# Two attention decodes on one core: last scores of a chunk ahead of the value matmuls, and a loop head of the tensor engine without its pin

## The chip, the cores and the metric

The kernel runs on one core of a Trainium2 chip. The metric is the device time of one execution in microseconds (us); I give medians of several executions. Profile times are counted from the start of the span, which is some 1.8 us shorter than the device time of the same execution.

## The reference, cut to what matters

Two single-token attention decodes with batch 4 and head size 128, their outputs side by side:

```python
def _A_ref(x, k_cache, v_cache, wq, wo):        # 32 query heads, 8 key heads, last W = 2048 of 8192 rows
    q = (x @ wq) ...
    scores = einsum("bhqd,bhkd->bhqk", q, k) * Dh ** -0.5
    o = einsum("bhqk,bhkd->bhqd", softmax(scores), v)
    return o.reshape(B, Sq, Hq * Dh) @ wo
def _B_ref(...):                                # the same, 32 key heads, all 8192 rows
    ...
return concatenate([_A_ref(...), _B_ref(...)], axis=-1)
```

"A" is the sliding-window part, "B" the block-cached one. Together they read 587 MB from memory, nearly all of it keys and values of B.

## The kernel before

The work is cut into 72 chunks: 8 of A, then 64 of B. A chunk of B is two heads of one batch row: 128 key tiles and 128 value tiles of 128x128, 4 MB each. For each chunk the tensor engine transposes the key tiles in groups of eight, another engine copies (evacuates) each group from `tr`, a PSUM tile of this kernel, to `kt` (one copy takes 691 ns on the vector engine and 1023 ns on the scalar engine, by the page of before), and the tensor engine multiplies the group with the query (scores). The values of the chunk before are multiplied in the second half of a chunk. Every engine's list of operations is written out by one Python program; repeating stretches, two chunks long, are then turned into loops of the engine's program. So the tensor engine has two loops, one in A (3 turns) and one in B (32 turns).

```python
def keys_part(c):
    if c % 2 == 0: sch.mark()                  # a loop turn begins here
    for g in range(ch["NG"]):                  # 16 groups in B
        emit_T(ch["s"] + g)                    # 8 transposes, then the evacuation on DVE or ACT
        if g >= SLAG: emit_S(ch["s"] + g - SLAG)   # scores, two groups behind (SLAG = 2)
        ...

def values_part(c, nxt):                       # values of chunk c, and the last two score groups of nxt
    late = list(range(ch["s_last"] + 1 - SLAG, ch["s_last"] + 1))
    todo = {2: lambda: emit_S(late[0]), 5: lambda: scores_last(nxt)} if ch["ab"] == 1 else {...}
    if ch["ab"] == 1:
        todo[10] = lambda: stats_gmax(nxt)                      # maximum over all partitions
        todo[14] = lambda: (stats_bc(nxt), exp_B(nxt))          # broadcast it, exponentials on ACT
    ...
    for g in range(16):
        emit_pv(c, g)                          # 8 value matmuls
        if g in todo: todo[g]()

for c in range(NC):
    if c == NCA: finish_A()                    # between the two loops
    keys_part(c)
    values_part(None if c == 0 else NONE if c == NCA else c - 1, c)
norm_sum(NC - 1); emit_wol()                   # after the loops: sums, output weights,
for g in ...: emit_pv(NC - 1, g)               # values of the last chunk, output
...
sch.emit_looped("pe", e, sems, loop_on(mybir.EngineType.PE, (0, 0)))   # head slots of the two loops
```

In the profile's lines `tr` are the transposes, `sc` the scores, `po` the value matmuls, `ms` small matmuls for maxima, broadcasts and sums, `pbb` the exponentials of B and `fin` the output product; DVE and ACT are the vector and the scalar engine, PEld the tensor engine's weight loads, and SP issues the loads.

A head slot of 0 pins the loop's first instruction to the start of a 256-instruction block of the engine's program; the padding ahead of it is jumped over. The traces show: an instruction packet is 16 KB (17 of them are 0.28 MB on the page of before); stalls by issue in the first passes fall 256 instructions apart. Loads are all issued by one queue, two buffers each for the keys and the values of B: a key load waits for the transposes of two chunks earlier, a value load for the value matmuls of two chunks earlier.

## Time and profile before

| | before |
|---|---|
| median of the first three runs | 1381.0 us (1378.02 to 1381.39) |
| span of the profiled run | 1378.8 us |
| tensor engine busy (PE, matmuls) | 1179.7 us, 86% |
| data queue, share of the 16 DMA engines | 99.4% |
| mean rate | 426 GB/s |

Read it with the DMA first. A load queue that is busy 99.4% of the span leaves only those places where it is not full, and the ends, where no load hides what is done. A tensor engine busy at 86% looks like a near second, but its idle time in the middle is waiting for keys (153.3 us in 58 waits in all). The prediction shows the lines for it.

### The profile page before, as it was taken

Reading aid. Unit: us, or ns where it says so; the run is one execution under the profiler, and the core shown is the slowest. Engines: PE = TensorE matmul, PEld = TensorE weight load, DVE = VectorE, ACT = ScalarE, POOL = GpSimd, SP = SyncE. Lnnn points to the kernel's source line nnn. Section 1 sums busy time; section 2 is a strip of 40 time slices with the busy share of each in tenths; the row PEclk is TensorE's granted clock in tenths of the full one; section 3 lists DMA queues with packets and bytes.
Section 4 is the critical chain, followed back from the end, with each engine's and each line's share of the span. In section 5 each row is a group of like instructions: output and inputs, shape, how many; then the busy total and the mean of one; then the engine's idle time right before and its main releaser. Section 6 shows DMA issues by size and latency. Waiting matters only on the chain.

```text
span 1378.8 us, 59836 instructions
## 1 busy us (share of the span) xinstructions
PE 1179.7 (86%) x27000; PEld 1137.7 (83%) x27001; DVE 656.7 (48%) x1434; ACT 434.8 (32%) x650; POOL 7.3 (1%) x28
## 2 busy tenths in 40 slices
PE   4896898888889888988889888988898889888988
PEld 4885898888888888888888888888887879787987
DVE  1674464444445444444445444444454445444543
ACT  1552333233223322332233233323232323232332
POOL 2000000000000000000000000000000000000000
PEclk9897999999999999999999999999999999999998
DMA  9999999999999999999999999999999999999997
GB/s 400 424 424 432 384 430 436 426 438 429 431 433 427 433 431 435 429 432 433 428 433 434 427 437 429 433 429 432 435 429 435 427 433 432 430 434 430 434 424 318
DMA packets 25254, 587.55 MB, mean 426 GB/s; under 512 B 2816, under 2 KB 2832, under 8 KB 6288
## 3 DMA queue, kind: packets, MB, share of 16 engines
q1 hardware_dynamic: 25208, 587.22, 99.4%
q8 instruction: 17, 0.28, 0.1%
q14 instruction: 5, 0.04, 0.0%
q10 hardware_dynamic: 24, 0.01, 0.0%
HBM read 587.21 MB, written 0.01 MB: 426 GB/s over the span
## 4 chain that ended last, share of the span: by engine, by line
DMA 61%; PE 36%; DVE 1%; issue 1%; ACT 0%; SPq 0%; DVEq 0%; ACTq 0%
DMA kv<-in_B_k_cache_dram 56%; PE tr L406 22%; PE sc L408 9%; PE po L408 2%; DMA kv<-in_B_v_cache_dram 2%; DMA kv<-in_B_wq_dram 2%; PE fin L408 2%; DMA kv<-in_A_k_cache_dram 1%; PE ms L408 1%; DVE sA L525 1%; ACT pba L595 0%; DVE rm L534 0%; DVE sA L523 0%; PE ms L406 0%; DVE zA L681 0%
## 5 line engine op out<-in xcount | busy, mean ns | idle before, releaser
L406 PE MATMUL tr<-identb,kv 128*128 128x128 bf16 x8704 | 701.5, 231 | 163.4 <-DMA kv<-in_B_k_cache_dram 153.3
L476 DVE COPY kt<-tr 128x1024 bf16<-128x1024 bf16 x736 | 502.7, 691 | 454.7 <-PE tr L406 450.2
L406 PEld LDWEIGHTS tr<-identb,kv 128*128 128x128 bf16 x8704 | 555.2, 104 | 186.2 <-DMA kv<-in_B_k_cache_dram 96.0
L474 ACT ACTIVATE kt<-tr 128x1024 bf16<-128x1024 bf16 x352 | 359.3, 1023 | 629.3 <-PE tr L406 629.1
L408 PE MATMUL sc<-qb,kt 128*128 128x64 bf16 x8704 | 449.5, 197 | 0.6 <-DVE gx L555 0.6
L408 PEld LDWEIGHTS sc<-qb,kt 128*128 128x128 bf16 x8704 | 371.8, 101 | 3.4 <-DVE gx L555 1.1
L408 PE MATMUL po<-pbb,kv 128*128 128x64 bf16 x8320 | 296.5, 192 | 6.6 <-issue 3.6
L408 PEld LDWEIGHTS po<-pbb,kv 128*128 128x128 bf16 x8320 | 269.5, 97 | 9.0 <-issue 3.7
L575 ACT ACTIVATE pbb<-sc,negb 64x128 bf16<-64x128 f32 x128 | 51.0, 399 | 298.3 <-DVE negb L562 297.5
L539 DVE TENSOR_REDUCE rm<-sc 64x1 f32<-64x128 f32 x128 | 36.9, 288 | 97.3 <-PE sc L408 96.4
L551 DVE TENSOR_REDUCE gm<-ms 1x2 f32<-1x128 f32 (+1 forms) x72 | 20.1, 279 | 48.5 <-PE ms L406 48.5
L562 DVE COPY negb<-ms 128x1 f32<-128x1 f32 (+1 forms) x72 | 11.4, 158 | 50.2 <-PE ms L408 50.2
L408 PE MATMUL ms<-identf,gx 1*128 1x1 f32 (+1 forms) x144 | 27.5, 258 | 0.8 <-DVE zA L681 0.8
L408 PEld LDWEIGHTS ms<-identf,gx 1*128 1x128 f32 (+1 forms) x144 | 21.4, 185 | 4.7 <-DVE zA L681 0.9
L575 ACT ACTIVATION_READ_ACCUMULATOR pbb<-sc,negb 64x1 f32 x128 | 23.7, 185 | 0.0
L406 PE MATMUL ms<-identf,rm 128*1 128x128 f32 (+1 forms) x72 | 19.7, 274 | 3.4 <-DVE rm L534 3.3
L408 PE MATMUL po<-pba,kv 128*128 128x64 bf16 x512 | 20.3, 199 | 1.6 <-ACT pba L595 1.0
L408 PEld LDWEIGHTS po<-pba,kv 128*128 128x128 bf16 x512 | 17.9, 102 | 4.5 <-ACT pba L595 3.8
L408 PE MATMUL fin<-wos,zB 128*4 128x512 bf16 x64 | 19.0, 378 | 0.0
L555 DVE TENSOR_SCALAR gx<-gm 1x128 f32<-1x128 f32 (+1 forms) x72 | 15.9, 221 | 2.5
L681 DVE CAST zB<-ms 64x8 bf16<-64x8 f32 x64 | 10.5, 163 | 8.9 <-PE ms L408 8.5
L408 PE MATMUL ms<-xT,kv 128*128 128x4 bf16 x256 | 7.1, 166 | 8.2 <-DMA kv<-in_A_wq_dram 4.5
(61 smaller groups left out, 168.1 us busy)
## 6 DMA issues: line engine op xcount, KB each, us to landing
kv<-in_B_k_cache_dram SPq DMA_DIRECT2D x63, 4096.0 KB, 27.2
kv<-in_B_v_cache_dram SPq DMA_DIRECT2D x63, 4096.0 KB, 31.9
kv<-in_A_k_cache_dram SPq DMA_DIRECT2D x8, 2048.0 KB, 13.0
kv<-in_A_v_cache_dram SPq DMA_DIRECT2D x8, 2048.0 KB, 14.8
kv<-in_A_wq_dram SPq DMA_DIRECT2D x1, 4096.0 KB, 12.4
kv<-in_B_wq_dram SPq DMA_DIRECT2D x1, 4096.0 KB, 27.3
wor<-in_A_wo_dram SPq DMA_DIRECT2D x8, 512.0 KB, 9.5
wos<-in_B_wo_dram SPq DMA_DIRECT2D x16, 256.0 KB, 20.4
```

What stands on the lines that cost most here:

```text
L406: sch.add("pe", lambda e: e.transpose(o, l, r), waits, key)
L408: sch.add("pe", lambda e: e.matmul(o, l, r, start=start, stop=stop), waits, key)
L474: sch.add("act", lambda e: e.activation(dst, src, ACTF.Copy), waits=waits, key=("ev", s))
L476: sch.add("dve", lambda e: e.tensor_copy(dst, src), waits=waits, key=("ev", s))
L525: emit = lambda e, src=src, b=b: e.scalar_tensor_tensor(out=t, in0=src, scalar=mk[:, b:b + 1], in1=t, op0=ALU.mult, op1=ALU.add)
L539: sch.add("dve", lambda e, src=src, pp=pp: e.tensor_reduce(out=rm[pp, m, 0:1], in_=src, axis=AX.X, op=ALU.max), waits=[("S", ch["s_last"]) ...
L551: sch.add("dve", lambda e: e.tensor_reduce(out=gm[0:C, m, 0:U], in_=src, axis=AX.X, op=ALU.max), waits=[("trm", c)], key=("gmax", c))
L555: sch.add("dve", lambda e: e.tensor_scalar(out=dst, in0=gv, scalar1=-scale, scalar2=None, op0=ALU.mult), waits=[("gmax", c)], key=("gx", c))
L562: sch.add("dve", lambda e: e.tensor_copy(negb[:, m, 0:C], ms[:, col:col + C]), waits=[("bc", c)], key=("negb", c))
L575: sch.add("act", lambda e, src=src, pp=pp, n=n, u=u: e.activation(probs_of(c)[pp, :, u], src, ACTF.Exp, bias=negb[pp, m, 0:1], scale=scale ...
L681: sch.add("dve", lambda e, src=src, pp=pp: e.tensor_copy(z[pp, :].rearrange("p (r b) -> p r b", r=k), src), waits=[("sm", c)] + free if h ...
```

## The change

The intent is twofold. First, in B, the last two score groups go ahead of most of the value matmuls, and with them the maximum and the exponentials, so that they are ready sooner. Second, the head of the tensor engine's A loop is no longer pinned, and lies wherever the instructions ahead of it end.

```diff
             late = list(range(ch["s_last"] + 1 - SLAG, ch["s_last"] + 1))
-            todo = {2: lambda: emit_S(late[0]), 5: lambda: scores_last(nxt)} if ch["ab"] == 1 else {0: lambda: emit_S(late[0]), 1: lambda: scores_last(nxt)}
             if ch["ab"] == 1:
-                todo[10] = lambda: stats_gmax(nxt)
-                todo[14] = lambda: (stats_bc(nxt), exp_B(nxt))
+                emit_S(late[0])
+                todo = {1: lambda: scores_last(nxt), 6: lambda: stats_gmax(nxt), 10: lambda: (stats_bc(nxt), exp_B(nxt))}
+            else:
+                todo = {0: lambda: emit_S(late[0]), 1: lambda: scores_last(nxt)}
...
-            sch.emit_looped("pe", e, sems, loop_on(mybir.EngineType.PE, (0, 0)))
+            sch.emit_looped("pe", e, sems, loop_on(mybir.EngineType.PE, (None, 0)))
```

## The prediction

Its sum: 1381.0 us, less 1.3 for the order, less 2.5 for the loop head (0.65 x 3.9), is 1377.2. What stands in it of fetching comes from counting in the trace of before: after five stalls the next fetch began 3.6 to 4.5 us later; the "3.6 to 5 us" and the range of slots from 100 to 240 are my estimates from that.

> **What bounds the kernel now.** I read the page first, its slices and its chain, then the stretches of time, then the waits of the tensor engine and the end of the chain in order of time.
>
> ```profile
> PEclk9897999999999999999999999999999999999998
> DMA  9999999999999999999999999999999999999997
> GB/s 400 424 424 432 384 430 436 426 438 429 431 433 427 433 431 435 429 432 433 428 433 434 427 437 429 433 429 432 435 429 435 427 433 432 430 434 430 434 424 318
> ...
> q1 hardware_dynamic: 25208, 587.22, 99.4%
> ```
>
> The data queue is busy 99.4% of the span and moves 424 to 438 GB/s in nearly every slice. 587.2 MB at the 431 GB/s of the long middle is 1362 us of the 1378.8 us span. So only three places are left for a gain: the start (slice 0), slice 4 with 384 GB/s, and the end (slice 39, 318 GB/s). The stretches, as a table, put numbers on the last two:
>
> ```profile
> 137.00:171.00 34.00, 29.85 (x709) 28.84 (x705) 16.29 (x35) 10.38 (x17) 0.00 (x0) 0.95 0.94 382
> 171.00:231.00 60.00, 59.60 (x1493) 58.00 (x1490) 34.37 (x73) 22.16 (x31) 0.00 (x0) 1.00 1.00 431
> 231.00:1330.00 1099.00, 948.00 (x21847) 921.97 (x21847) 517.21 (x1093) 337.35 (x504) 0.00 (x0) 0.93 1.00 431
> ```
>
> The columns are the stretch, its length, busy time of PE, PEld, DVE, ACT and POOL, the granted clock, the DMA share and GB/s. From 231 to 1330 us the tensor engine is busy 948 of 1099 us and idles 151 us; the DMA never idles (share 1.00). The chain agrees: 55.7% of the span is waiting for key loads of B. From 137 to 171 us the DMA delivers 382 instead of 431 GB/s: 34 x (431-382)/431 = 3.9 us of transfer lost. That is the passage from the sliding-window chunks (A) to the block-cached ones (B). The end, in the chain:
>
> ```profile
> 1330.26 31.64 DMA kv<-in_B_v_cache_dram
> ...
> 1363.40 0.43 PE sc L408 x8
> ...
> 1365.11 0.43 PE sc L408 x8
> ...
> 1368.88 0.32 PE ms L408 x2
> ...
> 1369.89 0.46 ACT pbb L575 x2
> ...
> 1371.66 3.76 PE po L408 x128
> ```
>
> Columns: start, duration, what. The values of the last but one chunk land at 1361.9 us. Then the tensor engine does 128 value matmuls of that chunk, the last two score groups (8 matmuls, 0.43 us each), waits for the exponentials, and does the last 128 value matmuls. This end runs on the tensor engine, not on the DMA.
>
> [...] the instruction queue (17 packets, 0.28 MB on the page) makes no block transfer from 72 to 123.5 us, then one at 126.1 us, while the tensor engine stands still from 123.53 to 128.96 us. [...] the trace shows clock 0.50 from 1361.1 to 1367.9 us.
>
> **Part one: order of scores and values.** For every B chunk the second to last score group moves from after three value groups to before the first, the last from after group 5 to after group 1, the global maximum from 10 to 6, and the broadcast with the exponentials from 14 to 10. No instruction is added or removed. The distances between dependent steps stay nearly the same (last scores to maximum: 5 groups either way; maximum to broadcast: 4). The first moved group needs an evacuation which ends about 1.0 us after its transposes; at the old place it had long been done, at the new one it may cost some 0.1 us per chunk. In the middle this goes into the 151 us of idle time, some 2.6 us for each of 57 chunks (1099 us at 19.4 us a chunk). Key buffers are freed by transposes, which do not move; value buffers by the last value matmul, before which as much work stands as ever. So loads are issued at the same times and **the middle gains 0**.
>
> At the end it gains: the first score group (0.43 us) is done while the engine waits for the values (it idles 1358.9 to 1361.9), and the exponentials get five value groups, 40 matmuls, behind which to hide instead of one. They take from the end of the broadcast at 1369.2 to 1370.36, some 1.2 to 1.5 us with the broadcast's copy; 40 matmuls take 40 x 31 ns = 1.25 us at full clock and 2.1 us at half. The wait of 0.98 us (value matmuls done about 1369.41, next matmul 1370.39) shrinks to 0 to 0.3. Sum 0.43 + 0.85 = **1.3 us**. The last values have landed by 1370.3, so the shortened end runs into no new wait.
>
> **Part two: the loop head.** The pin to slot 0 of a fetch block is taken off the A loop; the B loop keeps it. What does this do? A fetch starts about 3.6 to 5 us after the block before it is entered (five stalls that end with a fetch show 3.6 to 4.5 us until the next fetch begins). Counting rows of the tensor engine: the A loop has 859 instructions, what follows it up to the branch to the B loop 175. With the A head at slot 0 the branch sits at 859 + 175 = 1034 = 4 x 256 + 10: the last block is entered only 10 instructions before the jump, so the block of the B head is asked for just as it is needed. Hence the stall:
>
> ```profile
> PE tr L406 <- issue: 6.0, 2, 5.4
> ```
>
> That is, in the waits of the stretch from 100 to 175 us: 6.0 us over 2 times, 5.4 us the longest. This one stall delays the first transposes of B, the key load they release is issued at 141.12 us, and the DMA runs dry: the one hole of 3.9 us above. The first B keys had landed at 123.3 us, so without the stall the engine could start at once.
>
> If the A head starts elsewhere, at slot s, the branch sits at s + 1034, and the block is entered s + 10 instructions before it. For s between roughly 100 and 240 that is 2 us of sequencer time or much more, and the fetch is hidden wholly or mostly. The 5.4 us go, the first loads of B are issued about 4.5 us earlier, and **the hole closes: 3.9 us**, all of it on the path, as the DMA is what limits the rest. Where s is I can only estimate from the times of the early fetches: the block before the A head was entered some 230 to 255 instructions ahead of it. If s is so near to the end of the block that head and boundary coincide, nothing changes. I give 0.65 to the hole closing: 0.65 x 3.9 = **2.5 us** expected.
>
> **Rivals.**
> First, the loads stay as they are, the unpinned head falls on the old place or only the stall's place moves, and just the end gains: 1381.0 - 1.3 = 1379.7 us. For it: my count of s comes close to the boundary. Against it: the pin would then have been without effect.
> Second, the moved scores wait for the evacuation, the tensor engine becomes the bound and loads go out later: at 0.1 us for 64 chunks, 6 us slower if all were exposed. Against it: 2.6 us idle per chunk, and loads that take 27 to 32 us from issue to landing, two to three deep.
> Third, a tensor engine kept busier and earlier scores help the middle: PE busy 86% could tempt one to expect several per cent. Against it: DMA share 1.00 at 431 GB/s over 1099 us.
> Fourth, the clock: at the end the half clock lasted 6.8 us. [...] if the end is at half clock for 3.4 us, it is about 1.5 us shorter, in either kernel. This goes into the range.
>
> **Range and chances.** 1381.0 - 1.3 - 2.5 = 1377.2; I say 1377.0 us. With the hole closed 1375.8, without 1379.7; the three runs of before spread over 3.4 us (1378.02 to 1381.39), so 1373.0 to 1381.0 should hold it 8 times in 10. Two per cent are 27.6 us, seven times all that I found to win: faster 0.01, within 0.98, slower 0.01.
>
> **What would show it.** Part two right: between 120 and 135 us no 5 us stall by issue before the first B transposes, and 137 to 171 us at about 430 GB/s. Wrong: the stall stands, or another of its size shows up in the A chunks. Part one right: one score group before the wait for the last-but-one values, and under 0.3 us between the last value matmul of that chunk and the sums. The middle should show the same 431 GB/s and the same 19.4 us per chunk. The prediction fails if the key loads are issued later in the middle and the DMA share drops below 1.00, or if the middle moves at another GB/s than before.

## The result, and the profile after

The changed kernel takes 1375.43 us (median of 6 runs, 1374.3 to 1375.56); before, over six runs, 1379.64 us. The ratio is 0.9968, 95% interval 0.9955 to 0.9981. (Ratios here are the mean time of one kernel's runs over that of the other's of the same rounds, so not quite the ratio of the medians.) By this ratio it is 4.4 us less, clear of noise, within 2%. The profiled span fell by 5.1 us, from 1378.8 to 1373.7 us.

The page of the changed kernel, rate in the 40 slices and the queue of instruction blocks:

```profile
GB/s 401 423 424 433 426 434 426 437 429 433 429 433 429 432 429 434 428 434 428 434 428 434 429 435 431 431 431 431 431 431 432 430 432 430 432 430 432 430 427 338
...
q8 instruction: 16, 0.26, 0.1%
```

Slice 4 now moves 426 GB/s in place of 384. One block of instructions fewer is fetched, 16 in place of 17. The stretches of the changed kernel, same columns as in the prediction:

```profile
137.00:171.00 34.00, 27.64 (x604) 26.48 (x601) 13.86 (x31) 8.98 (x15) 0.00 (x0) 0.90 1.00 427
171.00:231.00 60.00, 58.84 (x1460) 56.64 (x1457) 33.54 (x74) 22.05 (x34) 0.00 (x0) 1.00 1.00 432
231.00:1325.00 1094.00, 950.31 (x21733) 917.51 (x21734) 515.66 (x1087) 336.45 (x500) 0.00 (x0) 0.93 1.00 431
```

The hole from 137 to 171 us is gone, and the middle moves the same 431 GB/s. What became of the stall ahead of the first B transposes is seen in the order of time (start, duration, the instructions, and in brackets the idle time before them and what ended it), first the kernel before, then the changed one:

```profile
128.97 0.50 PE L406 MATMUL tr<-identb,kv 128*128 128x128 bf16 x3 [5.43 <-issue]
```
```profile
123.41 0.79 PE L406 MATMUL tr<-identb,kv 128*128 128x128 bf16 x11 [0.72 <-DVE outsb L716]
```

The first B transposes start 5.6 us earlier, as soon as their keys have landed. The key load that they release is issued at 134.07 us in place of 141.12 us. From there the lead can be followed by the start of the first transposes of each chunk: chunk 16 starts at 271.32 us in place of 274.31 (3.0 us earlier), chunk 44 at 820.08 in place of 822.97, chunk 70 at 1329.32 in place of 1332.10 (2.8 us). So the middle neither adds to it nor takes much of it.

The remaining 2.3 us of the span come after the values of the last but one chunk have landed. The end of the chain of the changed kernel (start, duration, what):

```profile
1359.14 0.65 PE po L408 x16
1359.79 0.43 PE sc L408 x8
...
1363.78 0.31 PE ms L408 x2
1364.09 1.27 PE po L408 x40
1365.36 0.31 PE ms L408 x2
...
1366.56 3.76 PE po L408 x128
```

One score group stands among the value matmuls in place of two, and forty value matmuls follow the broadcast in place of eight; the sums (`ms`, 1365.36) follow them directly, where there had been 0.98 us of waiting for the exponentials. But 0.43 + 0.98 is 1.4 us, not 2.3. The experiments show where the rest comes from.

One new wait came with the order. In the waits of the changed kernel (total, times, longest):

```profile
PE sc L408 <- ACT kt L474: 12.8, 63, 0.2
```

The moved score group waits 0.2 us for its evacuation in nearly every chunk. The middle does not show it: there the engine waits for keys anyway (133.2 us in 57 waits in all).

### The profile page after: what moved, and what is told of

Read it like the earlier page. It is cut to its first block, busy times and chain, and to the rows that moved or that the text cites. A ratio compares the mean times of both kernels' runs of the same rounds, so it can differ in the third digit from the quotient of the medians.

```text
span 1373.7 us, 59835 instructions
## 1 busy us (share of the span) xinstructions
PE 1184.8 (86%) x27000; PEld 1134.7 (83%) x27001; DVE 656.5 (48%) x1434; ACT 434.8 (32%) x650; POOL 7.3 (1%) x28
## 4 chain that ended last, share of the span: by engine, by line
DMA 59%; PE 37%; DVE 2%; issue 1%; ACT 1%; SPq 0%; DVEq 0%
DMA kv<-in_B_k_cache_dram 54%; PE tr L406 22%; PE sc L408 9%; PE po L408 3%; DMA kv<-in_B_v_cache_dram 2%; DMA kv<-in_B_wq_dram 2%; PE fin L408 2%; DMA kv<-in_A_k_cache_dram 1%; PE ms L408 1%; DVE sA L525 1%; ACT kt L474 0%; DVE rm L534 0%; ACT pba L595 0%; DVE sA L523 0%; PE ms L406 0%
## 5 line engine op out<-in xcount | busy, mean ns | idle before, releaser
L406 PE MATMUL tr<-identb,kv 128*128 128x128 bf16 x8704 | 696.7, 230 | 138.1 <-DMA kv<-in_B_k_cache_dram 133.2
L408 PE MATMUL po<-pbb,kv 128*128 128x64 bf16 x8320 | 285.6, 192 | 6.9 <-issue 4.9
L408 PEld LDWEIGHTS po<-pbb,kv 128*128 128x128 bf16 x8320 | 264.8, 97 | 9.3 <-issue 5.1
L664 DVE TENSOR_TENSOR oz<-po,rz 128x8 bf16<-128x8 f32 x33 | 5.5, 167 | 41.5 <-PE po L408 41.5
```

The costliest lines, as they stand in the source:

```text
L406: sch.add("pe", lambda e: e.transpose(o, l, r), waits, key)
L408: sch.add("pe", lambda e: e.matmul(o, l, r, start=start, stop=stop), waits, key)
L664: sch.add("dve", lambda e: e.tensor_tensor(out=o, in0=i0, in1=i1, op=ALU.mult), waits=waits, key=("oT", c))
```

## The experiments

### The two parts, each alone

`order_only` is the changed kernel with the A loop pinned again:

```diff
-            ... loop_on(mybir.EngineType.PE, (None, 0))
+            ... loop_on(mybir.EngineType.PE, (0, 0))
```

> New order of scores, statistics and values, A loop still pinned to slot 0. My theory: the 5.4 us stall by issue ahead of the first B transposes stands, 137 to 171 us stays at about 382 GB/s, the first transposes of chunk 16 start at about 274 us as before, and only the end is shorter, by 1.4 us (0.43 for the score group, 0.98 for the wait for exponentials), up to 2.3 us if the half clock of the end happens to last 3.4 us. Time 0.9983 to 0.9990 of before. Rival (the order does it all, by earlier loads): 0.997 of before and the hole closed.

Measured: 1378.37 us against 1379.58 us of before in this batch, ratio 0.9992 (0.9978 to 1.0006). By time alone it is not separable from before; the profile decides. Waits of the tensor engine from 100 to 175 us:

```profile
PE tr L406 <- issue: 7.1, 2, 5.4
```

The stall of 5.4 us stands, 137 to 171 us moves 389 GB/s, and chunk 16 starts at 274.24 us, as before. Only the end is shorter: from the landing of the last but one values to the end of the span 14.6 us in place of 16.9 (how much of this is the clock, the section on the end tells).

`unpin_only` is the kernel before with `(None, 0)` for the loop heads and the old order.

> Old order, A loop unpinned. My theory: no stall by issue of several us ahead of the first B transposes (they start at about 123.4 us when their keys land), 137 to 171 us at about 427 GB/s, chunk 16 starts 3.0 us earlier than before (271.3 us), the end as before: one score group between the value groups and about 1 us of waiting for exponentials. Time 0.9978 of before. Rival (the loop head does nothing): 1.000.

Measured: 1376.27 us, ratio 0.9979 (0.9965 to 0.9992). Its stretch from 137 to 171 us:

```profile
137.00:171.00 34.00, 27.57 (x577) 26.53 (x574) 13.13 (x30) 7.96 (x14) 0.00 (x0) 0.85 1.00 427
```

The hole is gone, the first B transposes start at 123.61 us and chunk 16 at 271.42 us. So the loop head, and not the order, closes the hole. The product of the two ratios, 0.9992 x 0.9979 = 0.9971, meets the whole change's 0.9968.

### Is it the place of the block boundary?

Three kernels put the A head at other slots. Counting instructions between the stalls of the changed kernel (they fall 285, 541 and 797 instructions after the A head, 256 apart) puts its unpinned head at slot 256 - 29 = 227. The first two of these experiments keep the old order; pinned to 32 and to 128, the same edit as above with another number.

> Old order, A loop pinned to slot 32 in place of 0, so that the block ahead of the B head is entered 42 instructions before the jump in place of 10. My theory (a fetch is asked for on entering the block before it and takes some 6.5 us to be usable): the stall ahead of the first B transposes shrinks from 5.4 to about 2.5 us, and the hole of the DMA shrinks with it, time 0.998 to 0.9995. Rival (any pinned head makes the jump miss, [...]): 5.4 us as before.

The 6.5 us of this theory are an estimate from the trace of before, where stalls by issue at boundaries 256 instructions apart end at 61.44 and 67.85 us, and at 142.28 and 148.93 us: 6.4 and 6.65 us from one to the next. That a fetch is asked for on entering a block is my reading of the 3.6 to 4.5 us above.

Measured: 1374.88 us, ratio 0.9967 (0.9951 to 0.9982). Waits of the tensor engine from 100 to 175 us:

```profile
PE tr L406 <- DMA kv<-in_B_k_cache_dram: 1.3, 1, 1.3
```

No stall by issue is left ahead of the first B transposes. The wait of 1.3 us ends with the landing of the last of the keys, at 124.55 us, late in this run. The block of the B head was fetched from 121.35 us on, 4.8 us earlier than with slot 0. The trace files also record the branch to the B head, which no view lists: it took 6.84 us before, 5.99 in `order_only`, 2.16 here, 0.38 with slot 128 (the next run) and 0.31 with no pin. So a stall near the 2.5 us of the theory is still there, but it ran while the engine was busy to 123.4 us and then lacked keys. From 137 to 171 us 417 GB/s move, and chunk 16 starts at 271.18 us, as with no pin. So a pin is no trouble in itself: 32 more instructions between the boundary and the jump are enough here. The rival fails: with the loop still pinned, the branch takes 2.16 us and not 6.84.

This kernel has the old order, and its ratio of 0.9967 equals the 0.9968 of the whole change. By time alone, then, the loop head could be all of the gain; what the order adds only the profiles of the end show.

> Old order, A loop pinned to slot 128: the block is entered 138 instructions before the jump. My theory: stall under 0.7 us, the first B transposes start at 123.4 to 124 us, time as the unpinned one, 0.998 of before. Rival (the jump over padding itself costs the stall): 5.4 us as before.

Measured: 1377.24 us (1376.54 to 1381.23), ratio 0.9992 (0.9977 to 1.0007). Half of the theory held: no stall of several us ahead of B, 137 to 171 us at 428 GB/s. The first B transposes start at 125.12 us, when their keys have landed, as the loads had gone out later. But the gain is not there. The waits of the tensor engine from 40 to 100 us, for this kernel and then for the kernel before, tell where it went:

```profile
PE tr L406 <- issue: 2.1, 1, 2.1
...
PE sc L408 <- issue: 1.3, 1, 1.3
```
```profile
PE po L408 <- issue: 0.6, 1, 0.6
PE tr L406 <- issue: 0.6, 1, 0.6
```

With its head in the middle of a block, the A loop reaches the next boundary after 128 instructions by count, and its first turn has a stall of 2.1 us, then one of 1.3; that the block came too late there is my reading of them. The A key load that follows is issued at 58.4 us in place of 55.8. In A, too, the DMA has little in reserve; its rate from 60 to 96 us is 413 GB/s in place of 426, which is 36 x 13 / 426 = 1.1 us, and chunk 16 starts at 273.04 us, 1.6 us later than with no pin. Here the place of the head trades the stall at the B entry for stalls in the first turn of A; slots 227 and 32 avoid both large ones (their longest stall by issue in that turn is 1.1 us).

Last, `slot227` pins the changed kernel to the slot that I had counted.

> The changed kernel with the A loop pinned to slot 227, which my count of its stalls gives as the slot that it has without a pin. Same layout, so: 16 instruction packets, stalls of the tensor engine at the same instructions as in the changed kernel (285, 541 and 797 after the A head), first B transposes at 123.4 us, same time. If the count is wrong by more than a few slots, the stalls fall on other instructions or the A chunks lose a microsecond or two as with slot 128.

Measured: 1375.22 us, ratio 0.9970 (0.9955 to 0.9986), 16 instruction blocks, stalls by issue 541 and 797 instructions after the A head (the one at 285 does not stand out here). The count is right.

It also tells why the fetch is hidden without a pin, and this is not quite what the prediction said. The stall at 797 comes before the end of the loop's 859 instructions: the loop's own first turn already enters the block that holds the branch to B (1024 - 227 = 797). In the changed kernel that stall ends at 68.7 us, a block is fetched at 73.03 us, and then none until 126.09 us, after the first B transposes at 123.41. So the block of the B head had been there for 50 us. By these counts that would hold for every slot from 165 (1024 - 859) on, an estimate of which only 227 was run. With slots 32 and 128 the fetch came later, at 121.35 and 121.48 us, but ahead of the 126.14 us of slot 0; there, by the counts, it is the distance to the jump that does it.

### Why does B keep its pin?

`free` takes the second pin away as well: `(None, None)` on the changed kernel.

> The changed kernel with the B loop's head unpinned too. By my count the head then lies at slot 237 of a block and its 1607 instructions spread over 8 blocks in place of 7. [...] every turn of the loop fetches anew: instruction packets on the page go from 16 to 60 or more, the tensor engine stalls by some us each turn, time 1.000 to 1.02 of before where its 5 us of idle time a turn no longer hide it. Rival ([...] the loader moves the head): 16 or 17 packets and the time of the changed kernel.

Measured: 1522.59 us, ratio 1.1021 (1.0994 to 1.1047). I had expected 2% at most. From the page of this kernel, data queue and instruction queue:

```profile
q1 hardware_dynamic: 25208, 587.22, 91.9%
q8 instruction: 151, 2.47, 0.6%
```

and from its waits of the tensor engine:

```profile
PE tr L406 <- issue: 175.2, 37, 7.2
PE po L408 <- issue: 90.2, 34, 3.8
```

The times of the fetches show a pattern. Every second turn of the B loop fetches nine blocks anew and takes 52 to 56 us; the turns between fetch none and take 32 to 35 us (15 x 9 = 135 = 151 - 16; the expectation had every turn fetching). In a turn that fetches, the tensor engine stands still for up to 7.2 us several times, and the data queue falls to 91.9%: key loads wait for the transposes. In the changed kernel, where the B head is pinned, the page has 16 packets in the instruction queue (q8), and none falls between 168 and 1368 us: the turns of the loop's 1607 instructions, seven blocks by count, ran without a fetch there. Here, by my count, the body lay over eight blocks in place of seven; that it is this one block more that makes it refetch fits the count, but why only every second turn does so, and how the engine replaces blocks, is not shown.

### The end: order, or clock?

The control is the changed kernel itself.

> The changed kernel again, as the control of this batch: 0.9968 of before, hole closed, from the first value matmul of the last but one chunk to the first of the last chunk 7.3 us when the end has 3.4 us of half clock, some 5.6 us when it has none, 8.3 us when it has 6.8 us. If the half clock of the end is chance, this profile may differ from the first one there and nowhere else.

Measured: 1375.29 us, ratio 0.9963 (0.9950 to 0.9977). Its profile has 3.4 us of half clock at the end again, and 7.01 us where 7.3 were expected for that. `scores_only` moves the two score groups, but leaves maximum and exponentials at 10 and 14; the A loop is unpinned:

```diff
-                todo = {1: lambda: scores_last(nxt), 6: lambda: stats_gmax(nxt), 10: lambda: (stats_bc(nxt), exp_B(nxt))}
+                todo = {1: lambda: scores_last(nxt), 10: lambda: stats_gmax(nxt), 14: lambda: (stats_bc(nxt), exp_B(nxt))}
```

> A loop unpinned, score groups at their new places, maximum and exponentials at their old ones (10 and 14). My theory: hole closed; at the end the score group before the value wait saves 0.43 us and the wait for exponentials of about 1.0 us stays; first value matmul of the last but one chunk to the first of the last: 6.9 - 0.4 = 6.5 us at full clock (unpinned with the old order: 6.9 us), 8.2 us with 3.4 us of half clock. Time 0.5 to 1.0 us over the changed kernel. Rival (the early scores are all of the end's gain): as the changed kernel.

Measured: 1375.47 us, ratio 0.9966 (0.9953 to 0.9980), not separable from the control by time. Now the stretch from the first value matmul of the last but one chunk to the first of the last chunk, for five kernels in this order: before, unpinned alone, scores alone, pinned to 227 (new order), and the changed kernel. The second column is its length, the third from the end the granted clock:

```profile
1361.94:1371.50 9.56, 8.63 (x153) 7.97 (x155) 1.58 (x7) 1.14 (x5) 0.00 (x0) 0.69 0.85 350
```
```profile
1359.13:1366.01 6.88, 6.02 (x153) 5.35 (x154) 1.58 (x7) 1.14 (x5) 0.00 (x0) 1.00 0.97 402
```
```profile
1359.38:1366.03 6.65, 5.79 (x146) 5.11 (x146) 1.58 (x7) 1.14 (x5) 0.00 (x0) 1.00 0.97 404
```
```profile
1359.45:1365.15 5.70, 5.62 (x151) 5.10 (x148) 1.63 (x8) 1.14 (x5) 0.00 (x0) 1.00 0.97 400
```
```profile
1359.14:1366.39 7.25, 7.18 (x144) 6.60 (x146) 1.58 (x7) 1.13 (x5) 0.00 (x0) 0.76 0.91 377
```

At full clock the old order needs 6.88 us and the new one 5.70: in this stretch the order is worth 1.2 us. Of these the earlier scores are 0.23 us (6.88 to 6.65; eight matmuls at full clock), the earlier exponentials 0.95 us. The clock is worth more: the same old order took 9.56 us at 0.69 and 6.88 at 1.00, the same new order 7.25 at 0.76 and 5.70 at 1.00. So of the 2.3 us that the two first profiles differ by in this stretch, 1.2 are the order and 1.1, by subtraction, are the half clock, which lasted longer in the profiled run of before. In the trace files the half clock comes in records of 3.41 us or whole multiples of it (up to 17.07 us, the kernel before at 115.2 us; only a last record, cut off by the end of the trace, is shorter), and at the end they lie differently: from 1361.07 us for 6.83 us in the kernel before, from 1359.64 us for 3.41 us in the changed kernel, and none in the stretches at clock 1.00. What makes the clock fall is not shown; the tensor engine had not been idle throughout: it was busy 1.2 us of the 3.41 us ahead of the fall in the kernel before, and 1.15 us in the changed one. How much idle time it takes is not shown either.

The span does not keep all of the 1.2 us. From the landing of the last but one values to the end of the span, at full clock, the old order takes 14.3 us (`unpin_only`, and `slot32` and `slot128` too) and the new one 13.8 (`slot227`, and `warm`, which comes below). The chain shows why, first for `unpin_only`, then for `slot227`:

```profile
1366.17 3.76 PE po L408 x128
```
```profile
1368.96 0.42 PE po L408 x8
```

In the old order the last 128 value matmuls run through. In the new one, at full clock, the last eight of them wait for the last piece of the last load, which lands at 1368.91 us. Both kernels with the new order and full clock end 3.9 us after that landing. So of the order's 1.2 us the span keeps 0.5, by two profiles against three.

`warm` tests whether the idle time ahead of the last but one values brings the half clock. It repeats the first moved score group in odd chunks, writing the same numbers again:

```diff
...
-                emit_S(late[0])
+                for again in range(4 if nxt % 2 else 0, -1, -1):
+                    emit_S(late[0], again > 0)
```

The part cut here gives `emit_S` its second argument, with which only the last repetition signals that it is done.

> The changed kernel, with the first moved score group done five times over in every odd chunk (same numbers written again, 32 needless matmuls, about 1.0 us) ahead of the wait for values. If the half clock of the end comes from the idle time of 2.1 us ahead of the last but one values, it is gone here: idle 1.1 us, clock 1.00 to the end, 5.6 us from the first value matmul of that chunk to the first of the last, time 1.0 to 1.7 us under the changed kernel. Rival (the clock falls for another reason, or 1 us of needless work is not hidden at the passage to the B chunks and reopens a hole of 1 us or so): equal or slower.

Measured: 1374.49 us (1374.32 to 1374.68), ratio 0.9957 (0.9943 to 0.9971), against 1375.03 to 1375.52 us of the control on the same chip: no overlap, 0.8 us faster, the lowest ratio. Two of the first six runs of the changed kernel, in another batch, were as fast (1374.3 and 1374.44 us), so this kernel reaches steadily what the changed one reaches at times. In its profile the clock is 1.00 in the stretch above, which takes 5.71 us, and the needless matmuls are hidden (231 to 1325 us at 431 GB/s, 137 to 171 us at 427). One profile at full clock proves little, as two kernels above had that without help; that all five times lie under all five of the control says more, and `warm_pieces` below, the same but for the last load, had full clock there too. That the needless work keeps the clock up is likely, not proved. The gain is smaller than the 1.0 to 1.7 us expected, as the bound seen in `slot227` comes up here too. The chain of the warm kernel:

```profile
1330.96 38.01 DMA kv<-in_B_v_cache_dram
...
1369.01 0.42 PE po L408 x8
```

The last eight value matmuls now wait for the last piece of the last load, which lands at 1368.97 us.

### Is the cutting of the last load that new bound?

`warm_pieces` is the warm kernel, `pieces_only` the changed one, with three pieces in place of five:

```diff
-LASTV = (64, 32, 16, 8, 8)
+LASTV = (64, 32, 32)
```

> The warm kernel with the last value load cut into 64, 32 and 32 tiles in place of 64, 32, 16, 8 and 8. In the warm kernel the chain's end is no longer the tensor engine but the last piece of 8 tiles, landing at 1368.97 us while the DMA moves only 43 to 254 GB/s in the last 4 us. If the small pieces make that slow end, the last piece lands some 1 to 2 us earlier here, the last 128 value matmuls take 3.8 us in place of 4.6, and the time is 0.5 to 0.9 us under the warm kernel's 0.9957 of before. Rival (the 16 engines end unevenly whatever the pieces): equal, or slower since 32 tiles must land whole.

Measured: 1375.12 us, ratio 0.9969 (0.9955 to 0.9983): no gain over the warm kernel's 0.9957 (of another batch, and the intervals overlap). The profile decides: the last piece lands at 1368.85 us, no earlier, and now 32 tiles wait for it:

```profile
1368.85 0.05 issue
1368.89 1.13 PE po L408 x32
```

The rival was right. The landings of one piece on the 16 DMA engines lie 3.4 to 3.7 us apart in both kernels, whatever its size, and those of the 4 MB load before it as well (at the end of the stream of the kernel before it was 1.5 us, of `slot128` 3.8), so the slowest engine sets the end; with small pieces less work waits for it.

> The changed kernel with the last value load in 64, 32 and 32 tiles. There the last value matmuls start 1.2 to 1.7 us later and do not wait for the pieces, so: the time of the changed kernel, 0.9963 to 0.9968 of before, within 0.3 us. Rival (the small pieces hold up other loads too): 0.5 us faster or more.

Measured: 1375.28 us, ratio 0.9970 (0.9957 to 0.9984), as the changed kernel, as expected: there the tensor engine comes later than the pieces.

## Why the prediction was right

The range held (1373.0 to 1381.0), and the time came 1.6 us under the point given. Of these, 1.4 us are chance in the starting point: the prediction counted from 1381.0 us, and over six runs the kernel before has a median of 1379.64. Between the medians the gain was 4.2 us where 4.0 were given. Step by step:

- **The middle gains nothing.** Right: 431 GB/s before and after, and a lead of 3.0 us at chunk 16 that is 2.8 us at chunk 70. The second rival (scores waiting for the evacuation) came true as a wait, at twice the 0.1 us, and cost nothing, as the idle time of the middle took it. A chunk takes 19.6 us (822.97 - 274.31 over 28 chunks) and not 19.4. The argument rests on the DMA share of 1.00 at 431 GB/s; that no higher rate can be had there was not shown.
- **The loop head.** The mechanism was right in its main point: the fetch ahead of the B head began too late (at 126.14 us, with the branch begun at 121.77), and moving the boundary away from the jump removes the stall (5.4 us; with slot 32, fetched from 121.35 us on, none by issue is left there). What hides the fetch at slot 227 was not foreseen: the loop's first turn already brings the block. The size was somewhat off: 3.9 us for the hole, where the lead is 3.0 us, though the key load that the first transposes release went out 7.1 us earlier and not 4.5. About 0.3 us is that the stretch without the hole moves 427 and not 431 GB/s. The rest fits the spread of the 16 DMA engines. Added up over the DMA records, the changed kernel is 3.6 us of transfer ahead at 171 us and 3.3 us at 1320 us, but a chunk waits for the last engine, and for the last but one value load the 16 landings lie 3.5 us apart in place of 1.7. Why they spread is open. The chance of 0.65 multiplied this to 2.5 us, so the two errors nearly met; that is luck.
- **Where the head lies.** The estimate, 230 to 255 instructions after the boundary, was a little over the truth of 227. The claim that any slot from 100 to 240 would win was wrong: slot 128 hides the fetch at the B entry and loses 1.6 us in the A chunks. I had looked at one end of the loop only.
- **The end.** 1.3 us predicted, 1.2 us at equal clock in the stretch shown. Its parts were off: the score group is worth 0.23 us at full clock and not 0.43, the exponentials 0.95 and not 0.85. That the shortened end would run into no new wait held in the first profile of the changed kernel, but not at full clock, where the wait for the last piece leaves 0.5 us of the gain.
- **The clock.** It differed between profiles at the end, as the range allowed for, and it was worth more than given: 1.55 us between clock 0.76 and 1.00, 2.7 between 0.69 and 1.00. That its place is chance was my estimate; it is not shown.

What stays open: what the order is worth in unprofiled runs, as no time here separates it (`order_only` 0.9992, interval 0.9978 to 1.0006), and how often the end falls into the half clock in unprofiled runs. The old order without the hole spread from 1374.7 to 1377.7 us (`unpin_only`, `slot32`), the changed kernel from 1374.3 to 1375.6; a shorter idle time ahead of the last values may be why, which is not shown, as the clock of the end is known for profiled runs only.

## What to carry to other kernels

When the DMA is full, look for the places where it is not, and for the end after the last load; an order that gave the engines more air elsewhere was worth nothing there (431 GB/s before and after). A loop head's place in the instruction blocks cost microseconds here at the entry of the next loop (5.4 us with slot 0) and in the first turn (2.1 and 1.3 us with slot 128), and a large body that by count touched one block more cost them in every second turn (turns of 52 to 56 us in place of 32 to 35), so count instructions to the next boundary before moving or freeing a pin. Compare short ends of a kernel at equal granted clock, or a difference of the clock is taken for a gain (here 1.1 us of 2.3).
